# First pair of a hash-attention kernel: the queries' hash products moved ahead of the keys' transposes, and the first key block's scores cut into equal halves

## The chip, the cores and the metric

The kernel runs on one core of one Trainium2 chip. The time is the device time of one execution in microseconds (us); a kernel's time is the median of several executions. The profile is one execution recorded by the hardware profiler; its times start at the first instruction.

The engines are named as in the profile: PE is TensorE's matrix multiplication and PEld its weight load, DVE is VectorE, ACT is ScalarE, POOL is GpSimd, SP is SyncE, which here only issues transfers.

## The reference

Attention over hash buckets (4 batches, 8 heads, 768 positions, head size 64), and behind it two dense layers with a squared ReLU between them. A query sees only the keys of its own bucket; the bucket is made of the signs of six products with `proj`.

```python
def _attn_ref(q, k, v, proj):
    ...
    q_bits = (np.einsum('bhsd,dk->bhsk', q, proj) > 0).astype(np.int64)
    k_bits = (np.einsum('bhsd,dk->bhsk', k, proj) > 0).astype(np.int64)
    ...
    mask = q_bucket[:, :, :, None] == k_bucket[:, :, None, :]
    scores = scale * np.matmul(q, k.transpose(0, 1, 3, 2))
    scores = np.where(mask, scores, -1000000000.0)
    scores = scores - np.max(scores, axis=-1, keepdims=True)
    attn = np.exp(scores)
    attn = attn / (np.sum(attn, axis=-1, keepdims=True) + 1e-09)
    return np.matmul(attn, v)

def _moe_ref(x, w_in, w_out):
    r = np.maximum(x @ w_in, 0.0)
    return (r * r) @ w_out
```

All inputs and the output are float32.

## The kernel before

The attention comes first, in 16 pairs of heads (`NP`). Each pair works on tiles of 128 partitions: head 0 of the pair lies on partitions 0 to 63, head 1 on 64 to 127. A pair has 768 queries and 768 keys; the keys are taken in six blocks of 128 (`kt`, 0 to 5). The two dense layers follow and make up most of the time. The order of the instructions on every engine is the order of the program's text: the whole of it stands under a manual schedule, and each engine works off its own queue.

What happens for one pair:

- `features` (or, for pair 0 alone, `first_features`) brings queries and keys into the form with the head's 64 numbers on partitions, `feat`. For pair 0 it is done by TensorE: three transposes of 128x128 into one tile `tp` for each half of 384 positions, copied out by ScalarE for the queries (`w == 0`, line 316) and by VectorE for the keys (`w == 1`, line 318).
- `hash_bits` multiplies `feat` by `projs` (line 346), for one half of 384 positions (`c`) and one head (`h`) at a time. It is float32, and each product shows as two passes in the trace. `projs` holds `proj` twice, once for each head; the two halves are loaded on SP's and ScalarE's queues behind the queries and keys of pair 0 (line 277).
- `signs` turns the products into query bits on ScalarE (line 356, four instructions, in the order half 0 head 0, half 0 head 1, half 1 head 0, half 1 head 1). The keys of pair 0 get theirs on VectorE, in `first_keys` (two comparisons at line 370, one multiply-add at line 374), one half of 384 keys at a time.
- `score(pr, kt)` multiplies one block of 128 keys by all queries (line 396): a product of features in float32 and a product of bits in bfloat16 into the same PSUM tile `st`, cut by `CUTS` into 512 and 256 queries. One exponential for each cut (line 413) writes the weights `e`, for both heads at once, so 1024 and 512 elements per partition. For the very first block the feature products of both cuts are issued first and the bit products behind them; in all others a cut's bits come first and its features next.
- `add_up`, `attend`, `sum_up` and `normalize` sum the weights, multiply them by the values and divide.

PSUM tiles come from a pool of three (`turn`): transposes, hash products and scores share them, and whoever asks for one waits until its last reader is done. The queries' hash products of pair 0 go instead into the tile `void` that `keep_busy` writes. `keep_busy` issues matmuls of a constant, eight ahead of the first transposes and two ahead of the keys' transposes.

Before the loop over the pairs the order was, on TensorE: eight matmuls of `keep_busy`, the queries' transposes (both halves), two matmuls of `keep_busy`, the transposes of key half 0, the queries' hash products, the hash products of key half 0, the transposes of key half 1. Then `score(0, 0)`, the hash of key half 1 (`first_keys(1, ...)`), `score(0, 1)`, and so on. On VectorE: the copy of key half 0, the three instructions for its bits, the copy of key half 1, then the bits of half 1, and then the transposes for pair 1.

Of the kernel before, what the change touches and what calls it, by code (L numbers as in the profile page):

```python
# [34 lines left out]
def kernel(  # L35
# [13 lines left out]
    B, H, S, D = q.shape  # L49
# [5 lines left out]
    HS = S // 2  # L55
# [5 lines left out]
    CUTS = (0, 512), (512, S)  # L61
# [42 lines left out]
    def turn(name):  # L104

        return ps_s.tile([P, 2, 512], FP32, name=name, tag="turn")
# [195 lines left out]
    def first_features(w, r):  # L302

        if r == 0:
            feat[0, w] = p_f.tile([P, S], FP32, name=f"feat{w}")
        tp = turn("tp")[:, 0]
        for i in range(SB // 2):
            t = r * (SB // 2) + i
            nc.tensor.transpose(  # L309
                out=tp[:, i * P:(i + 1) * P],  # L310
                in_=nat[0, ("q_nat", "k_nat")[w]][:, t].rearrange("p h d -> p (h d)"),
                identity=ident,
            )
        out = feat[0, w][:, r * HS:(r + 1) * HS]
        if w == 0:
            nc.scalar.copy(out=out, in_=tp[:, 0:HS])
        else:
            nc.vector.tensor_copy(out=out, in_=tp[:, 0:HS])

    busy = const.tile([P, 512], BF16, name="busy")  # L320
    void = ps_o.tile([P, 1024], FP32, name="xo")

    def keep_busy(n, w=512):

        for _ in range(n):
            nc.tensor.matmul(  # L326
                out=void[:, 0:w], lhsT=busy[:, 0:P], rhs=busy[:, 0:w], start=True, stop=True
            )
# [8 lines left out]
    def hash_bits(pr, banks, ws=(0, 1), cs=(0, 1)):  # L337


        for w in ws:  # L340
            hashed[pr, w] = banks
            for c in cs:
                g = 2 * w + c
                for h in range(2):
                    rows = slice(h * D, (h + 1) * D)
                    nc.tensor.matmul(  # L346
                        out=banks[g * NR_B:(g + 1) * NR_B, h, 0:HS], lhsT=projs[rows],
                        rhs=feat[pr, w][rows, c * HS:(c + 1) * HS], start=True, stop=True,
                    )

    def signs(pr, w):
        bits[pr, w] = t = all_bits[pr % 2][w]
        for c in range(2):
            at = slice((2 * w + c) * NR_B, (2 * w + c + 1) * NR_B)
            for h in range(2):
                nc.scalar.activation(  # L356
                    out=t[h * D:h * D + NR_B, c * HS:(c + 1) * HS], in_=hashed[pr, w][at, h, 0:HS],
                    func=ACTF.Sign, scale=HUGE, bias=lifts[at],
                )
# [26 lines left out]
    def score(pr, kt):  # L386

        e = ring[len(weights) % NRING]
        weights[pr, kt] = e
        key = slice(kt * P, (kt + 1) * P)  # L390
        sts = []

        def products(st, lo, hi, src, first):
            for h in range(2):
                rows = slice(h * D, (h + 1) * D)
                nc.tensor.matmul(  # L396
                    out=st[:, h, 0:hi - lo], lhsT=src[pr, 1][rows, key],
                    rhs=src[pr, 0][rows, lo:hi], start=first, stop=not first,
                )


        if (pr, kt) == (0, 0):
            for lo, hi in CUTS:
                sts.append(turn("st"))
                products(sts[-1], lo, hi, feat, True)
        for i, (lo, hi) in enumerate(CUTS):
            if len(sts) <= i:
                sts.append(turn("st"))
                products(sts[i], lo, hi, bits, True)
                products(sts[i], lo, hi, feat, False)  # L410
            else:
                products(sts[i], lo, hi, bits, False)
            nc.scalar.activation(  # L413
                out=e[:, :, lo:hi], in_=sts[i][:, :, 0:hi - lo], func=ACTF.Exp, scale=scale
            )
# [176 lines left out]
    with tc.manual_schedule():  # L592
# [10 lines left out]
        first_features(0, 0)  # L603
        first_features(0, 1)
        keep_busy(2)
        first_features(1, 0)
        hash_bits(0, void.rearrange("p (h c) -> p h c", h=2), (0,))
        signs(0, 0)
        first_keys(0, turn("hash"))
        first_features(1, 1)  # L610
# [3 lines left out]
        for pr in range(NP):  # L614
# [17 lines left out]
            if pr > 0:  # L632
                round_weight(b - 2)
                load_weight(b)
                for m in sums.get(pr, ()):
                    sum_in(m)
            score(pr, 0)
            if pr == 0:
                first_keys(1, turn("hash"))
            score(pr, 1)  # L640
            if pr == 0:
                for w in range(2):
# [8 lines left out]
            if pr == X_0 + 1:  # L651
                for n in range(2):
                    load_unit(n)
            part_weight(a)
            score(pr, 2)
            if pr == 0:
                prepare()
# [826 lines left out]
```

## Time and profile before

| | us |
|---|---|
| time, median of 4 runs | 878.47 |
| lowest and highest of them | 878.12, 879.19 |
| the profiled execution's own time | 878.54 |
| its span, first to last instruction | 876.8 |
| outside the span | 1.74 |
| PE busy between 13.0 and 28.6 us | 14.12 of 15.6 |
| ACT busy between 13.0 and 28.6 us | 14.85 of 15.6 |
| PE busy from 28.6 us to the end | 839.43 of 848.2 |

A line of the timeline gives the start, the duration, the engine, the source line, the operation, the tile written and those read, the shape, the count, and in brackets how long the engine was idle before it and what ended that idle time. Lines that follow each other closely are merged. The chain of waits is found backwards from the last instruction: at every step it goes to what released it. The end of a matmul is modelled by the profiler, and a wait for several things is charged to the one that seems to have come last.

### The profile page before, as it was taken

Reading aid. Unit: us, or ns where it says so; the run is one execution under the profiler, and the core shown is the slowest. Engines: PE = TensorE matmul, PEld = TensorE weight load, DVE = VectorE, ACT = ScalarE, POOL = GpSimd, SP = SyncE. Lnnn points to the kernel's source line nnn. Section 1 sums busy time; section 2 is a strip of 40 time slices with the busy share of each in tenths; the row PEclk is TensorE's granted clock in tenths of the full one; section 3 lists DMA queues with packets and bytes.
Section 4 is the critical chain, followed back from the end, with each engine's and each line's share of the span. In section 5 each row is a group of like instructions: output and inputs, shape, how many; then the busy total and the mean of one; then the engine's idle time right before and its main releaser. Section 6 shows DMA issues by size and latency. Waiting matters only on the chain.

```text
span 876.8 us, 12130 instructions
## 1 busy us (share of the span) xinstructions
PE 864.8 (99%) x4340; PEld 519.6 (59%) x4340; DVE 760.1 (87%) x1099; ACT 391.8 (45%) x673; POOL 107.4 (12%) x172
## 2 busy tenths in 40 slices
PE   8999999999999999999999999999999999999996
PEld 4444444444444444444688865556888755568885
DVE  5999999999999998888689978888889788888875
ACT  6988888888888851222211123332111233321110
POOL 2000000000000000554032021111000211110002
PEclk9999999999999999999999999999999999999999
DMA  9877967998888536999788874536756754355565
GB/s 169 151 150 133 234 155 153 183 258 223 180 179 218 167 102 213 297 265 285 296 297 259 219 169 160 175 121 222 282 157 182 166 166 154 124 168 158 154 178 102
DMA packets 224131, 167.09 MB, mean 191 GB/s; under 512 B 164448, under 2 KB 181344, under 8 KB 224064
## 3 DMA queue, kind: packets, MB, share of 16 engines
q1 hardware_dynamic: 189152, 87.19, 41.4%
q0 software_dynamic: 12528, 41.30, 15.4%
q10 hardware_dynamic: 22384, 37.76, 14.1%
q8 instruction: 36, 0.59, 0.3%
q14 instruction: 31, 0.25, 0.1%
HBM read 124.52 MB, written 41.68 MB: 190 GB/s over the span
## 4 chain that ended last, share of the span: by engine, by line
PE 96%; DVE 2%; ACT 1%; issue 0%; DVEq 0%; ACTq 0%
PE acc L712 40%; PE st L396 17%; PE acc L931 16%; PE xo L438 14%; PE acc L884 6%; PE hash L346 2%; PE tot L455 1%; DVE total L428 1%; ACT bits L356 1%; PE xo L326 0%; ACT e L413 0%; PE tp L309 0%; PE xo L477 0%; PE xo L346 0%; DVE x_t L493 0%
## 5 line engine op out<-in xcount | busy, mean ns | idle before, releaser
L413 ACT ACTIVATE e<-st 128x1024 f32<-128x1024 f32 x192 | 145.0, 810 | 44.8 <-PE st L396 41.0
L396 PE MATMUL st<-feat,feat 64*128 64x512 f32 (+1 forms) x768 | 150.4, 483 | 0.0
L438 PE MATMUL xo<-e,v_nat 128*64 128x512 f32 (+1 forms) x768 | 134.8, 492 | 0.0
L712 PE MATMUL acc<-b,leaf 128*128 128x256 f32 x600 | 132.9, 379 | 0.0
L712 PEld LDWEIGHTS acc<-b,leaf 128*128 128x128 f32 x600 | 113.9, 190 | 16.0 <-issue 0.6
L428 DVE TENSOR_TENSOR total<-total,e 128x1536 f32<-128x1536 f32 x64 | 112.4, 1756 | 8.2 <-ACT e L413 3.6
L438 PEld LDWEIGHTS xo<-e,v_nat 128*64 128x64 f32 x768 | 51.3, 136 | 82.2 <-issue 74.3
L931 PE MATMUL acc<-t_x,w_unit 128*128 128x512 f32 x192 | 90.2, 592 | 0.0
L396 PEld LDWEIGHTS st<-feat,feat 64*128 64x128 f32 x768 | 66.0, 188 | 32.8 <-issue 23.2
L712 PE MATMUL acc<-t,leaf 128*128 128x256 f32 x336 | 76.2, 380 | 0.0
L356 ACT ACTIVATE bits<-hash,lifts 32x384 bf16<-32x384 f32 x120 | 68.7, 573 | 2.3 <-PE hash L346 0.5
L712 PEld LDWEIGHTS acc<-t,leaf 128*128 128x128 f32 x336 | 63.6, 190 | 9.1 <-DVE t L516 0.5
L796 DVE SCALAR_TENSOR_TENSOR b<-h 128x512 f32<-128x512 f32 x96 | 65.7, 691 | 3.0
L396 PE MATMUL st<-bits,bits 64*128 64x256 bf16 (+1 forms) x384 | 63.2, 325 | 1.7 <-ACT e L413 1.2
L931 PE MATMUL acc<-x,w_unit 128*128 128x512 f32 x128 | 60.1, 592 | 0.0
L712 PE MATMUL acc<-x,w_unit 128*128 128x512 f32 x128 | 56.6, 594 | 0.0
L712 PE MATMUL acc<-b_t,leaf 128*128 128x256 f32 x240 | 53.8, 379 | 0.0
L931 PEld LDWEIGHTS acc<-t_x,w_unit 128*128 128x128 f32 x192 | 36.5, 190 | 28.9 <-issue 26.8
L719 ACT COPY two<-acc 128x256 f32<-128x256 f32 (+1 forms) x29 | 12.5, 432 | 87.7 <-PE acc L712 78.4
L719 ACT COPY one<-acc 128x256 f32<-128x256 f32 (+1 forms) x29 | 12.5, 431 | 84.2 <-PE acc L712 55.4
L712 PEld LDWEIGHTS acc<-b_t,leaf 128*128 128x128 f32 x240 | 45.5, 190 | 6.2
L396 PEld LDWEIGHTS <-bits 64*128 64x128 bf16 x384 | 23.6, 93 | 42.7 <-issue 38.6
(159 smaller groups left out, 1167.3 us busy)
## 6 DMA issues: line engine op xcount, KB each, us to landing
leaf<-w_out ACTq DMA_DIRECT2D x142, 256.0 KB, 3.1
w_unit<-w_in SPq DMA_DIRECT2D x16, 640.0 KB, 4.0
raw<-in_moe_w_in_dram SPq DMA_DIRECT2D x16, 512.0 KB, 5.5
raw<-in_moe_w_out_dram SPq DMA_DIRECT2D x16, 512.0 KB, 4.3
w_unit<-w_in SPq DMA_DIRECT2D x8, 896.0 KB, 8.1
w_out<-sums POOLq DMA_DIRECT2D x16, 448.0 KB, 6.9
sum<-w_in SPq DMA_DIRECT2D x16, 448.0 KB, 5.0
v_nat<-in_v_dram SPq DMA_DIRECT2D x16, 384.0 KB, 4.4
```

Of the source, the lines that this page charges most:

```text
L346: nc.tensor.matmul(out=banks[g * NR_B:(g + 1) * NR_B, h, 0:HS], lhsT=projs[rows], rhs=feat[pr, w][rows, c * HS:(c + 1) * HS], start=True, ...
L356: nc.scalar.activation(out=t[h * D:h * D + NR_B, c * HS:(c + 1) * HS], in_=hashed[pr, w][at, h, 0:HS], func=ACTF.Sign, scale=HUGE, bias=li ...
L396: nc.tensor.matmul(out=st[:, h, 0:hi - lo], lhsT=src[pr, 1][rows, key], rhs=src[pr, 0][rows, lo:hi], start=first, stop=not first,)
L413: nc.scalar.activation(out=e[:, :, lo:hi], in_=sts[i][:, :, 0:hi - lo], func=ACTF.Exp, scale=scale)
L428: nc.vector.tensor_tensor(out=totals[pr], in0=totals[pr], in1=weights[pr, kt][:, :, 0:S], op=ALU.add)
L438: nc.tensor.matmul(out=xo[h * D:(h + 1) * D, lo:hi], lhsT=nat[pr, "v_nat"][:, h, kt * D:(kt + 1) * D], rhs=weights[pr, kt][:, h, lo:hi], s ...
L455: nc.tensor.matmul(out=tot[g * 32:(g + 1) * 32, 0:HS], lhsT=ones, rhs=totals[pr][:, h, c * HS:(c + 1) * HS], start=True, stop=True,)
L712: nc.tensor.matmul(out=acc[to], lhsT=a(i), rhs=b(i), start=first and i == 0, stop=last and i == n - 1, skip_group_check=True,)
L719: nc.scalar.copy(out=t, in_=acc[of])
L796: nc.vector.scalar_tensor_tensor(out=out, in0=h, scalar=0.0, in1=h, op0=ALU.max, op1=ALU.mult)
L884: nc.tensor.matmul(out=out, lhsT=w[:, a], rhs=b, start=start, stop=stop, skip_group_check=True)
L931: nc.tensor.matmul(out=acc[to], lhsT=w[:, PLACE[a], f], rhs=bt[b](f), start=first and f == 0, stop=last and f == NFT // 2 - 1, skip_group_ ...
```

## The change

Two edits, both for pair 0 alone.

First, the call that makes the queries' hash products is moved up by one: it now stands ahead of the transposes of key half 0 instead of behind them. Nothing is added or left out; on TensorE four products change places with three transposes, and no other engine's order changes.

Second, the first key block (`kt` 0 of pair 0) is scored in two halves of 384 queries instead of 512 and 256. The four feature products, the four bit products and the two exponentials of that block have 384 columns (768 elements for an exponential) each. All other blocks keep `CUTS`. With it two waits for PSUM tiles change places in key block 1 and 2: the second tile of block 1 now waits for the second exponential of block 0, and the first tile of block 2 for VectorE's reading of the hash of key half 1; before, it was the other way about.

```diff
@@ score @@
+        cuts = CUTS
         if (pr, kt) == (0, 0):
-            for lo, hi in CUTS:
+            cuts = (0, HS), (HS, S)
+            for lo, hi in cuts:
                 sts.append(turn("st"))
                 products(sts[-1], lo, hi, feat, True)
-        for i, (lo, hi) in enumerate(CUTS):
+        for i, (lo, hi) in enumerate(cuts):
             if len(sts) <= i:
                 sts.append(turn("st"))
                 products(sts[i], lo, hi, bits, True)
...
         first_features(0, 0)
         first_features(0, 1)
         keep_busy(2)
+        hash_bits(0, void.rearrange("p (h c) -> p h c", h=2), (0,))
         first_features(1, 0)
-        hash_bits(0, void.rearrange("p (h c) -> p h c", h=2), (0,))
         signs(0, 0)
         first_keys(0, turn("hash"))
         first_features(1, 1)
```

`HS` is 384 and `S` is 768.

## The prediction

> **What bounds the kernel now.** I read the page first (busy shares and the chain that ended last), then the chain of waits in order of time for the stretch the change touches, then the timeline of the same stretch, and last the tile `projs`, because the moved products read it.
>
> ```profile
> span 876.8 us, 12130 instructions
> PE 864.8 (99%) x4340; PEld 519.6 (59%) x4340; DVE 760.1 (87%) x1099; ACT 391.8 (45%) x673; POOL 107.4 (12%) x172
> ...
> PE 96%; DVE 2%; ACT 1%; issue 0%; DVEq 0%; ACTq 0%
> ```
>
> TensorE is the bound: 99% busy, 96% of the chain. The edits add no work to it, so they count only through when the first scores are ready.
>
> ```profile
> 6.72 0.36 PE tp L309 x3
> 7.09 1.05 PE xo L346 x8
> 8.13 0.44 PE hash L346 x4
> 8.58 0.48 PE tp L309 x3
> 9.05 1.98 PE st L396 x10
> 11.03 0.02 issue
> 11.05 1.03 ACT e L413
> 12.09 0.04 issue
> 12.13 3.41 PE st L396 x24
> ...
> 21.27 1.51 ACT e L413 x2
> ```
>
> This is the chain from 6.72 to 22.78 us. Up to 12 us one thing follows another: key transposes, hash products, scores, first exponential. From 12.13 the exponentials and signs carry it (ScalarE is busy 14.85 of the 15.60 us between 13.0 and 28.6), and from 25.16 on it is TensorE to the end. No load interrupts that chain. So if the first exponential starts later, everything behind starts later by what reaches 12.13, unless a later wait has room.
>
> ```profile
> 6.54 0.31 PEld L309 LDWEIGHTS tp<-ident,k_nat 128*128 128x128 f32 x3 [0.31 <-DMA k_nat<-in_k_dram]
> 7.04 0.40 PEld L346 LDWEIGHTS xo<-feat,projs 64*32 64x32 f32 x8 [0.19 <-ACT feat L316]
> 7.13 0.56 DVE L318 COPY feat<-tp 128x384 f32<-128x384 f32 x1 [3.84 <-PE tp L309]
> 8.25 2.35 ACT L356 ACTIVATE bits<-xo,lifts 32x384 bf16<-32x384 f32 x4 [1.44 <-PE xo L346]
> 8.51 0.31 PEld L309 LDWEIGHTS tp<-ident,k_nat 128*128 128x128 f32 x3 [0.62 <-PE xo L346]
> 9.86 0.38 DVE L374 TENSOR_SCALAR bits<-bits,spans,bases 128x384 bf16<-128x384 bf16 x1
> 9.88 0.30 PEld L396 LDWEIGHTS st<-feat,feat 64*128 64x128 f32 x4 [0.59 <-DVE bits L370]
> 10.41 0.71 PE L396 MATMUL st<-bits,bits 64*128 64x512 bf16 x4
> ```
>
> Columns: start, duration, engine, line, operation, count, idle time before and its releaser. Line 1: the first key transposes start as `k_nat` lands. Line 2: the queries' products start at 7.04; the bracket blames ScalarE's copy, but the two copies ran 5.75 to 6.81 and were long done. The late one is a load:
>
> ```profile
> 1.86 0.58 SPq L277 DMA_DIRECT2D projs<-in_proj_dram  x1
> 1.99 0.57 ACTq L277 DMA_DIRECT2D projs<-in_proj_dram  x1
> DMA to landing us min/median/max: 5.1/5.2/5.3
> ```
>
> Issued at 1.86 and 1.99, landing 5.1 and 5.3 us later: 6.96 and 7.29. The products of head 0 need the first, those of head 1 the second (weight loads start at 7.04 and 7.29). The key transposes now lie wholly in that wait (6.54 to 7.09).
>
> **The change part by part.** *Products ahead of transposes.* TensorE issues in the program's order, so the three key transposes, ready at 6.54, go behind four products (eight passes) that cannot start before 7.04. The products gain nothing: `projs` lands when it did. They start their last pass at 7.65 as before, and the signs still run 8.25 to 10.60. The transposes' place: behind the other hash products, the last pass started at 8.09 and the transposes' weight load at 8.51, 0.42 later. I take that row: 7.65 + 0.42 = 8.07 instead of 6.54, +1.53. The lower bound is the row where scores follow transposes (8.78 to 8.98, 0.20): 7.85, +1.31.
>
> The Trainium skill, "TensorE: Matmul & The Clock Gate", Part 2 (step-by-step), says weight loads are pulled ahead of matmuls in flight when row groups don't conflict or the background buffer is free. By it the transposes could start soon after 7.65, some 0.4 us earlier, and the estimate would be 879.3; the row of 8.51 shows the load held back although the semaphore it is charged to came at the products' end, so the row is taken.
>
> What is queued behind the transposes moves with them, on TensorE and VectorE. Copy of key half 0: 7.13 to 8.65. Hash of that half: 7.74 to 9.27. Key bits ready: 9.86 + 0.38 = 10.24, so 11.77. Second transposes, first score products and VectorE's second copy move by the same 1.53 (copy ends 10.83, so 12.36). ScalarE's queue keeps its times until the exponential. No DMA moves: SP's queue has neither edit in it, and its transfers that wait for pair 0's buffers are issued from 11.45 and 18.04, the transposes being over at 10.6.
>
> *Halves.* The first key block is scored as 384 + 384 instead of 512 + 256: as many matmuls, columns and activations. The second score tile waits for the bank of the key hash, freed by VectorE: 9.88 + 1.53 = 11.41. Its passes are 384 columns instead of 256. A 512-column pass is 0.43 long (start to start), so 384 take 0.32; the first one behind fresh weights took 0.10 more (8.98 to 9.52). The bit products start at 11.41 + 0.42 + 0.32 = 12.15, behind the key bits of 11.77, so here TensorE decides. A bit product lasts 0.38 at 512 columns and 0.27 at 256, so 0.32: done 12.47, exponential at 12.50 instead of 11.05, +1.45. The signs (10.60) no longer hold it.
>
> Here the halves give something back. The first exponential has 768 elements instead of 1024. No row shows 768; the bounds are 0.59 (512) and 1.03 (1024), and I take the middle, 0.81. It frees its bank at 13.31, and the next scores start at 13.36 instead of 12.13: +1.23. The hash of key half 1 lies in between: 12.15 + 0.32 = 12.47, last pass 0.35 later and 0.32 long, so over by 13.15, hidden with 0.2 to spare. Without that cover (0.59 for the exponential) it would decide and the shift be about 1.0. At 1.03 it is 1.45.
>
> Two waits change place. The second tile of key block 1 now waits for the second exponential (12.50 + 1.51 = 14.01; needed 13.20 + 1.23 = 14.43), and the first of block 2 for VectorE's reading of the second key hash (13.07 + 1.41 = 14.48; needed 13.75 + 1.23 = 14.98). Both have 0.4 or more to spare: nothing. VectorE's transposes for pair 1 end 15.24 + 1.41 = 16.65; pair 1's hash wants them at 15.50 + 1.23 = 16.73. That costs nothing, but with under 0.1 to spare.
>
> **Sum:** -0 (products not earlier) + 1.53 (transposes) - 0.08 (signs no longer awaited, TensorE now) - 0.22 (shorter first exponential) = +1.23 on the profiled execution's 878.54, so 879.77. Its time is 0.07 above the median 878.47, so 879.7 for a median. With the bounds, +0.8 to +1.6: 879.2 to 880.1 is the forecast's own range.
>
> **Rivals.**
> *A, the keys land last (not slower).* If `k_nat` landed 1.5 us later, at 8.07 or after, the transposes would lose nothing by standing behind the products, and only the halves would act. Key bits are ready at 10.24, the first half starts 10.41, exponential at 10.77 instead of 11.05: -0.3, 878.2. For it: these loads land 3.7 to 5.2 us after issue, a wide spread. Against: in the trace the keys came 0.45 before the first `projs`, and `projs` is issued behind them on the same two queues. 8%.
> *B, the delay is swallowed later.* There are idle stretches on TensorE at 20.81 (0.48), 24.16 (0.99) and a hold for VectorE near 32.4 (0.27). Against: the first two wait for ScalarE, which shifts too; the third waits for a VectorE queue that itself waited for an exponential at 22.8. 878.5; 6%.
> *C, the delay grows (clearly slower).* The spare of under 0.1 us at pair 1's transposes fails and every bound is at its far end: first exponential 1.03, VectorE 1.45 late plus 0.3 to 0.5 of waits that no longer interlock. +1.8 to 2.2: 880.5. For it: VectorE is busy without a break from 13.0 to 17. Against: each step has its row. 17%.
> *D, TensorE falls to half pace.* At the start, 512-column matmuls of `busy` are 0.42 apart, and 0.21 from 6.13 on. The change opens idle stretches at 6.72 to 7.07 and 8.65 to 9.27. If they brought the slow pace back, some 3 us of passes between 9.27 and 14 would double: +4.2, 882.7. Against: after the idle 0.99 us before 25.16 passes run at the same pace as before it. The granted clock shows 1.00 throughout, the slow start included, so only durations can tell. 5%.
>
> **How the numbers follow.** Forecast 64%, A 8%, B 6%, C 17%, D 5%. The predicted time is the forecast's, 879.7. What a measurement of this kernel can tell from no change is 0.2%, 1.76 us: faster needs under 876.7, slower over 880.2. The forecast, A and B lie between; so "same" though I expect a real loss of about 0.14%. Slower: C's larger part, D, and a few per cent of the forecast's tail, 22%. Faster has no mechanism larger than 0.3 us: 2%. The range 878.6 to 881.0 holds forecast, C, and part of A and B.
>
> **What would show it.** In the changed profile: the queries' products still start near 7.04 and their signs near 8.25 (first step); the first key transposes load at about 8.07 and VectorE copies at 8.65 (second); bit products near 12.15, behind VectorE's 11.77 (third); a first exponential of 0.81 at 12.50 and the next scores at 13.36 (fourth); pair 1's signs at 16.58 + 1.23 = 17.8 and TensorE's unbroken run from 26.4 instead of 25.16. It would be wrong if `projs` landed earlier, if the transposes didn't wait for the products, or if a shift seen at 13.4 were gone at 26.

## The result, and the profile after

The changed kernel takes 880.05 us (median of 39 runs, 879.40 to 880.93) against 878.69 us (59 runs) before: ratio 1.0015, 95% interval 1.0011 to 1.0020, so 1.0 to 1.8 us slower. The profiled execution took 879.65 us with a span of 877.9, against 878.54 and 876.8: 1.1 us more.

The page of the changed kernel, engines' busy time and the chain that ended last:

```profile
span 877.9 us, 12130 instructions
PE 864.9 (99%) x4340; PEld 519.1 (59%) x4340; DVE 760.1 (87%) x1099; ACT 391.5 (45%) x673; POOL 107.1 (12%) x172
...
PE 96%; DVE 2%; ACT 1%; DMA 1%; issue 0%; DVEq 0%; ACTq 0%
```

No engine has more work than before: as many instructions, TensorE's busy time up by 0.1 us. What is new is a share of 1% for a transfer in the chain, which had none. The chain of waits of the changed kernel, in order of time (start, duration, what), shows which:

```profile
1.86 5.07 DMA projs<-in_proj_dram
6.93 0.14 issue
7.07 1.04 PE xo L346 x8
8.11 0.49 PE tp L309 x3
8.60 0.02 issue
8.63 0.57 DVE feat L318
9.19 0.04 issue
9.24 0.84 PE hash L346 x4
...
13.38 3.41 PE st L396 x24
...
26.40 0.72 PE st L396 x6
```

The chain now begins with the load of `projs`, goes through the queries' products and only then comes to the key transposes. Before, transposes ran 6.72 to 7.08 on this chain and the products followed. The second score stretch starts at 13.38 instead of 12.13, and the run of TensorE that lasts to the end at 26.40 instead of 25.16.

From the timeline of the same stretch, changed kernel (lines between these are left out):

```profile
7.04 0.38 PEld L346 LDWEIGHTS xo<-feat,projs 64*32 64x32 f32 x8 [1.26 <-ACT feat L316]
7.07 1.04 PE L346 MATMUL xo<-feat,projs 64*32 64x384 f32 x8 [0.79 <-DMA projs<-in_proj_dram]
8.04 0.31 PEld L309 LDWEIGHTS tp<-ident,k_nat 128*128 128x128 f32 x3 [0.62 <-issue]
8.22 2.36 ACT L356 ACTIVATE bits<-xo,lifts 32x384 bf16<-32x384 f32 x4 [1.81 <-issue]
8.63 0.56 DVE L318 COPY feat<-tp 128x384 f32<-128x384 f32 x1 [5.34 <-PE tp L309]
11.36 0.38 DVE L374 TENSOR_SCALAR bits<-bits,spans,bases 128x384 bf16<-128x384 bf16 x1
12.13 0.49 PE L396 MATMUL st<-bits,bits 64*128 64x384 bf16 x4
12.52 0.81 ACT L415 ACTIVATE e<-st 128x768 f32<-128x768 f32 x1 [1.94 <-PE st L396]
12.55 0.83 PE L346 MATMUL hash<-feat,projs 64*32 64x384 f32 x4
13.31 0.16 PEld L396 LDWEIGHTS <-bits 64*128 64x128 bf16 x2 [0.62 <-issue]
13.38 0.39 PE L396 MATMUL st<-bits,bits 64*128 64x512 bf16 x2
...
15.79 0.94 DVE L333 STREAM_TRANSPOSE feat<-k_nat 128x768 f32<-128x768 f32 x1
...
16.72 0.91 PE L346 MATMUL hash<-feat,projs 64*32 64x384 f32 x16
```

The first two lines carry the result: moved to the front, the products start when they started before, 7.04, and TensorE sits idle for 0.79 us ahead of them, released by the landing of `projs`. That time held the key transposes. Everything from line 3 on is late, apart from the signs (8.22 against 8.25).

Where does the delay go afterwards? Matching the VectorE instructions of the two traces one to one gives a clean answer: the changed kernel is 1.24 us late at 24.5 us, 1.23 at 53, 1.23 at 158, 1.23 at 313, 1.22 at 415 and 1.22 at 827. The delay of the first pair is carried to the last VectorE instruction at 869 us without gain or loss; only behind it is 0.1 us made up, so that the spans differ by 1.1. The second trace of both edits carries its 1.42 us unchanged to 450 us, and then 0.2 us come in (see the last section). It had been expected that the delay would reach the dense layers unchanged to within 0.05 us, whatever the loads add: so far as the attention goes that held, beyond it it did not.

### The profile page after: what moved, and what is told of

Read it like the earlier page. It is cut to its first block, busy times and chain, and to the rows that moved or that the text cites. A ratio compares the mean times of both kernels' runs of the same rounds, so it can differ in the third digit from the quotient of the medians.

```text
span 877.9 us, 12130 instructions
## 1 busy us (share of the span) xinstructions
PE 864.9 (99%) x4340; PEld 519.1 (59%) x4340; DVE 760.1 (87%) x1099; ACT 391.5 (45%) x673; POOL 107.1 (12%) x172
## 4 chain that ended last, share of the span: by engine, by line
PE 96%; DVE 2%; ACT 1%; DMA 1%; issue 0%; DVEq 0%; ACTq 0%
PE acc L714 40%; PE st L396 17%; PE acc L933 16%; PE xo L440 14%; PE acc L886 6%; PE hash L346 2%; PE tot L457 1%; DVE total L430 1%; DMA projs<-in_proj_dram 1%; ACT bits L356 1%; ACT e L415 0%; PE xo L479 0%; PE xo L346 0%; DVE x_t L495 0%; DVE recs L489 0%
## 5 line engine op out<-in xcount | busy, mean ns | idle before, releaser
L415 ACT ACTIVATE e<-st 128x1024 f32<-128x1024 f32 (+1 forms) x192 | 145.1, 810 | 46.1 <-PE st L396 42.3
L396 PE MATMUL st<-feat,feat 64*128 64x256 f32 (+2 forms) x768 | 150.6, 484 | 0.0
L396 PE MATMUL st<-bits,bits 64*128 64x256 bf16 (+2 forms) x384 | 63.0, 325 | 1.4 <-ACT e L415 1.0
```

The costliest lines, as they stand in the source:

```text
L396: nc.tensor.matmul(out=st[:, h, 0:hi - lo], lhsT=src[pr, 1][rows, key], rhs=src[pr, 0][rows, lo:hi], start=first, stop=not first,)
L415: nc.scalar.activation(out=e[:, :, lo:hi], in_=sts[i][:, :, 0:hi - lo], func=ACTF.Exp, scale=scale)
```

## The experiments

In all tables "next scores" is the start of the first exponential of key block 1, the instruction that started at 13.42 us in the profile before and at 14.67 with the change; the "next scores" of the prediction are TensorE's, which began 1.29 us earlier in both (12.13 and 13.38). "Key transposes load" is the start of their first weight load. "Against before" is the difference of the medians, with the 95% interval of the ratio put into us.

| run | key transposes load | next scores | against before, us |
|---|---|---|---|
| before | 6.54 | 13.42 | |
| both edits | 8.04 | 14.67 (+1.25) | +1.36 (1.0 to 1.8) |
| both edits, again | 8.21 | 14.85 (+1.43) | +1.30 (0.5 to 2.1) |
| order alone | 8.09 | 14.77 (+1.35) | +1.19 (0.4 to 2.0) |
| halves alone | 6.84 | 13.73 (+0.31) | +0.06 (-0.6 to 1.0) |
| projs between, new order | 7.72 | 14.35 (+0.93) | +0.65 (0.0 to 1.6) |
| projs between, old order | 7.57 | 14.20 (+0.78) | +0.63 (-0.2 to 1.4) |
| keys' transposes together | 6.69 | 13.20 (-0.22) | +0.12 (-0.4 to 1.1) |
| the same, no halves | 6.67 | 13.62 (+0.20) | +0.44 (-0.4 to 1.2) |
| keys loaded first | 4.56 | 14.26 (+0.84) | +0.55 (-0.3 to 1.3) |
| projs on GpSimd, new order | 8.74 | 15.37 (+1.95) | +1.90 (1.1 to 2.7) |
| projs on GpSimd, old order | 6.82 | 13.69 (+0.27) | +0.30 (-0.6 to 1.0) |
| the same, keys' transposes together | 6.60 | 13.64 (+0.22) | +0.08 (-0.7 to 0.9) |
| no load of projs, new order | 7.28 | 13.91 (+0.49) | +0.25 (-0.4 to 1.2) |

The intervals are wide against the effects, so most verdicts below rest on the traces, where a start is known to 0.01 us, and the medians only say whether they fit. But there is one trace of each kernel, and executions differ: the two of both edits are 0.18 us apart at the next scores.

### Each edit alone

Order alone:

```diff
-        first_features(1, 0)
         hash_bits(0, void.rearrange("p (h c) -> p h c", h=2), (0,))
+        first_features(1, 0)
```

> The queries' hash products ahead of the keys' transposes, the first block in 512 and 256 as before. Theory (the transposes stand behind products that wait for projs, and the halves give a little back): first key transposes load near 8.05 us instead of 6.54, key bits 1.5 us later, next scores (12.13 before) near 13.6, as nothing shortens the first exponential: +1.4 to +1.5 us, so slightly worse than both edits together. Rival (the halves cost, the order is free because projs is late anyway): no change, within 0.3 us of before.

Halves alone is the changed kernel with these two lines put back.

> The first block in two halves of 384, the old order. Theory: the first exponential starts near 10.98 instead of 11.05 and is 0.81 instead of 1.03 long, the next scores start near 11.85 instead of 12.13, and pair 1's signs near 16.3 instead of 16.58: -0.25 to -0.3 us. Rival (the halves cost): +0.5 us or more, because the second tile's 128 more columns stand ahead of the bit products.

The order costs nearly everything by itself: +1.19 us, +1.35 in the trace, just under the expected 1.4 to 1.5. The rival, that the order is free, falls. But the theory had the halves give back 0.2, and of that little is left. Order alone, ScalarE:

```profile
12.41 1.51 ACT L413 ACTIVATE e<-st 128x1024 f32<-128x1024 f32 x2 [1.79 <-PE st L396]
```

Without the halves the first exponential starts at 12.41, although the loads came 0.05 us later than in the trace of both edits, where it starts at 12.52. The second score tile is a third shorter (256 columns instead of 384), so the bit products come earlier; the halves lose at the start of the exponential some 0.15 of the 0.22 us that they win by its length.

Halves alone measures no difference, 0.25 us being below what eleven runs tell. Its trace has the keys late by themselves:

```profile
6.84 0.57 PEld L309 LDWEIGHTS tp<-ident,k_nat 128*128 128x128 f32 x3 [0.40 <-DMA k_nat<-in_k_dram]
...
7.68 0.56 DVE L318 COPY feat<-tp 128x384 f32<-128x384 f32 x1 [4.41 <-PE tp L309]
...
13.73 2.65 ACT L415 ACTIVATE e<-st 128x1024 f32<-128x1024 f32 x3 [0.64 <-PE st L396]
```

The keys landed 0.30 us later than in the profile before (weights load at 6.84 against 6.54), and three transposes' weight loads took 0.57 instead of 0.31 us, since TensorE still ran at its slow pace. So VectorE's copy is 0.55 late (7.68 against 7.13), but the next scores only 0.31: from the copy on, the halves win 0.24 in the old order, as expected. One trace of each shows it; the medians don't.

### Which load comes first

Both kernels load `projs` between the queries and the keys of pair 0; the first has both edits, the second the halves and the old order.

```diff
             nat[0, name] = t
-        for h, queue in enumerate((nc.sync, nc.scalar)):
-            queue.dma_start(out=projs[h * D:(h + 1) * D, 0:NBITS], in_=proj)
+            if name == "q_nat":
+                for h, queue in enumerate((nc.sync, nc.scalar)):
+                    queue.dma_start(out=projs[h * D:(h + 1) * D, 0:NBITS], in_=proj)
```

> Both edits, and projs loaded between pair 0's queries and keys instead of behind the keys. Theory (of the 1.5 us by which the transposes are late, the wait for projs is 0.5): projs lands near 5 us, the products start near 6.4 to 6.8, the transposes at 7.4 to 7.8, if the keys have landed by then; the time is 0.3 to 0.7 us under that of both edits, so +0.6 to +1.0 against before. Rival (the load's place is of no account, the order of matrix work alone costs): same time as with both edits, +1.2 to +1.4.

> Halves, old order, and projs loaded between pair 0's queries and keys. Theory: the key transposes start when the keys land, now 0 to 0.7 us later than 6.54; the products follow without a wait. So -0.3 to +0.4 us against before, and the two orders differ by 0.4 to 1.1 us under this order of loads, against some 1.5 us under the old one. Rival (order of matrix work alone): the two orders still differ by 1.5 us.

The weight loads of the key transposes, new order and then old order:

```profile
7.72 0.31 PEld L310 LDWEIGHTS tp<-ident,k_nat 128*128 128x128 f32 x3 [0.76 <-DMA k_nat<-in_k_dram]
```

```profile
7.57 0.31 PEld L310 LDWEIGHTS tp<-ident,k_nat 128*128 128x128 f32 x3 [1.62 <-DMA k_nat<-in_k_dram]
```

In both the bracket now names the keys' load: `projs` lands near 5 us (3.1 to 3.7 after its issue at 1.49), and the keys about 1 us later than before, since their issue moved from 1.28 to 2.12. With the keys last the order of the matrix work is nearly free: the two kernels differ by 0.02 us in the medians and by 0.15 in the next scores, where under the old load order it is over 1 us. This is the prediction's rival A brought about on purpose: the keys land last (at 7.5 to 7.6, not at 8.07 as it asked, but `projs` is early too), and the order's cost goes. The new order's +0.65 lies in the expected 0.6 to 1.0, but partly by luck: its transposes waited for the keys, not for the products. That the old order would stay between -0.3 and +0.4 was a miss; it measured +0.63, because I had put the keys' lateness at 0.7 at most.

### How late projs is

Three kernels load `projs` on GpSimd's queue, right behind the identity matrix.

```diff
         make_identity(nc, ident)
+        for h in range(2):
+            nc.gpsimd.dma_start(out=projs[h * D:(h + 1) * D, 0:NBITS], in_=proj)
```

> Both edits, and projs loaded on GpSimd's queue right behind the identity, so without a place behind the queries and keys; the loads of queries and keys keep their queues. It takes the wait for projs out of the new order. Theory (the 1.5 us by which the key transposes are late are 0.53 of wait for projs, 0.58 of products, 0.42 until the transposes' weights load): if projs lands by 6, the products start near 6.4 to 6.7, the transposes 1.0 later, near 7.5, and the next scores are late by 0.6 to 0.8 instead of 1.23: +0.6 to +0.9 us. Rival (the whole cost is the wait for projs): no loss against before. Second rival (the wait costs nothing): +1.2 to +1.4 as with both edits.

> Halves, old order, projs on GpSimd's queue. Theory: the key transposes start when the keys land (about 6.5 to 6.8) and the products directly behind them; key bits as before or 0.1 earlier, the halves give 0.25: -0.2 to -0.4 us against before. If the order were free once projs is early, it would be equal to the run before this one; the theory has them 0.9 to 1.1 us apart.

> Halves, both halves of the keys transposed ahead of the products, projs on GpSimd's queue. Theory: as the run before it and 0.1 to 0.2 us better, since the second transposes and VectorE's second copy leave the stretch ahead of the first scores: -0.4 to -0.5 us, unless the keys land late. Rival (the second transposes now stand ahead of the products, which no longer wait): +0.2 us against the run before it.

All three expectations stood on an early landing and were missed, for it was later: issued at 1.78 and 2.48, landed 5.4 to 5.9 us after. The new order, timeline:

```profile
7.62 1.20 PE L344 MATMUL xo<-feat,projs 64*32 64x384 f32 x8 [0.77 <-DMA projs<-in_proj_dram]
7.97 0.15 PEld L344 LDWEIGHTS xo<-feat,projs 64*32 64x32 f32 x6 [0.25 <-DMA projs<-in_proj_dram]
8.74 0.31 PEld L307 LDWEIGHTS tp<-ident,k_nat 128*128 128x128 f32 x3 [0.62 <-issue]
```

The run tests the opposite of what was meant: a `projs` that comes still later. Head 1's weights load at 7.97 instead of 7.27, 0.70 us later, and the key transposes at 8.74 instead of 8.04, 0.70 later, and the next scores 0.70 later (15.37 against 14.67). Under the new order a late `projs` is passed on in full. The second trace of both edits has the same on a smaller scale (transposes 0.17 later, next scores 0.18). In the old order the same late load leaves the next scores at +0.27, though there too the chain of waits now runs through that load.

Then the load was taken away: `projs` is filled with the constant 0.5 in its six columns, so the buckets are not the reference's.

```diff
         nc.vector.memset(projs, 0.0)
+        nc.vector.memset(projs[:, 0:NBITS], 0.5)
-        for h, queue in enumerate((nc.sync, nc.scalar)):
-            queue.dma_start(out=projs[h * D:(h + 1) * D, 0:NBITS], in_=proj)
```

> Both edits, with projs filled with the constant 0.5 in place of proj, so no load of it at all: the buckets are not the reference's, the work on every engine is the same. It takes the wait for projs wholly out of the new order. Theory (1.53 us of delay = 0.53 wait + 0.58 products + 0.42 until the transposes' weights load): products start between 6.3 and 6.9, as ScalarE's copies end; transposes between 7.2 and 7.6, no longer tied to projs; offset of the dense layers +0.5 to +0.8 us instead of +1.23 to +1.41, time +0.5 to +0.9. If the whole cost is the wait: transposes at the keys' landing (6.5 to 6.8), time at or under that of before. If the wait costs nothing: +1.2 or more.

```profile
6.25 0.40 PEld L344 LDWEIGHTS xo<-feat,projs 64*32 64x32 f32 x8 [0.42 <-ACT feat L314]
...
7.28 0.31 PEld L307 LDWEIGHTS tp<-ident,k_nat 128*128 128x128 f32 x3 [0.62 <-DMA k_nat<-in_k_dram]
```

Now the products start at 6.25, on ScalarE's copies, and the transposes at 7.28: 0.76 of the delay at the transposes goes with the wait (7.28 against 8.04), and as much at the next scores (13.91 against 14.67). What stays, 0.49, is the products themselves and the pause behind them: the transposes still stand behind eight passes. (Their bracket names the keys' load, but it had landed by 6.7.) So neither "the whole cost is the wait" nor "the wait costs nothing" holds. The median, +0.25, is below the expected 0.5 to 0.9; its interval, -0.4 to 1.2, takes in the trace's 0.49, and no change as well, so this rests on the trace.

### Towards a better order

The first puts the second half's transposes into the wait for `projs`, with the halves; the second does the same without them.

```diff
         first_features(1, 0)
+        first_features(1, 1)
         hash_bits(0, void.rearrange("p (h c) -> p h c", h=2), (0,))
         signs(0, 0)
         first_keys(0, turn("hash"))
-        first_features(1, 1)
```

> Halves, and both halves of the keys transposed ahead of the queries' products, so in the wait for projs. Theory (work put into that wait costs nothing, and the second transposes and VectorE's second copy leave the stretch between the key hash and the first scores): if the keys land as in the profile of before, key bits stay at 10.24, the first exponential is at 10.77 instead of 11.05, the next scores at 11.65 instead of 12.13: -0.4 to -0.5 us, 0.2 better than halves alone. Rival (the first stretch is set by the loads' landing and nothing else): no change against halves alone.

> The same order with 512 and 256 in the first block. Theory: bit products at 10.41 to 10.65, held by VectorE's key bits (10.24) and ScalarE's signs (10.60) as before, so the first exponential stays at 11.05 and the time at that of before, within 0.15 us; what the free TensorE could give is only to be had with the halves. Rival: the transposes moved give 0.4 us by themselves.

The third also loads, transposes and hashes the keys ahead of the queries.

```diff
-        for src, name in ((q, "q_nat"), (k, "k_nat")):
+        for src, name in ((k, "k_nat"), (q, "q_nat")):
...
-        first_features(0, 0)
-        first_features(0, 1)
-        keep_busy(2)
         first_features(1, 0)
+        first_features(1, 1)
+        keep_busy(2)
+        first_features(0, 0)
+        first_features(0, 1)
+        first_keys(0, turn("hash"))
         hash_bits(0, void.rearrange("p (h c) -> p h c", h=2), (0,))
         signs(0, 0)
-        first_keys(0, turn("hash"))
-        first_features(1, 1)
```

> Halves, and the keys loaded, transposed, copied and hashed ahead of the queries; the queries' half-0 bits are enough for the first half. Theory (the keys' way to their bits is the longer one, so it should get the earlier load): key bits at 9.6 instead of 10.24, first exponential near 10.2 to 10.3, next scores near 11.1 instead of 12.13: -0.8 to -1.0 us. Rival (the queries' signs take over, as they start later): signs of half 0 end near 10.0 and hold the bit products: -0.3 to -0.5 us.

The first has the earliest next scores of all runs, 13.20, with keys that landed 0.15 later than in the profile before: half of the expected gain of 0.4 to 0.5. In the median it is told neither from before (+0.12) nor from halves alone. The second was to stay at the time of before; its first exponential came 0.21 later (11.26 for 11.05), and its +0.44 has too wide an interval to tell. The third is a plain miss. ScalarE, first kernel and then third:

```profile
8.47 2.36 ACT L356 ACTIVATE bits<-xo,lifts 32x384 bf16<-32x384 f32 x4 [1.58 <-PE xo L346]
10.93 1.51 ACT L415 ACTIVATE e<-st 128x768 f32<-128x768 f32 x2
```

```profile
9.53 2.36 ACT L356 ACTIVATE bits<-xo,lifts 32x384 bf16<-32x384 f32 x4 [0.99 <-issue]
11.91 1.51 ACT L415 ACTIVATE e<-st 128x768 f32<-128x768 f32 x2
```

Signs from 9.53 for 2.36 us end at 11.89, and the exponential starts 0.02 later without idle time; in the first kernel the two are 0.10 apart (10.83, 10.93). The halves need only the first two signs, but ScalarE works in order and the exponential stands behind all four. I had counted the bits of half 0 and not the queue.

But the exponential is not what makes the third kernel late. Its timeline and its chain of waits have TensorE and VectorE in that place:

```profile
10.06 1.56 PE L396 MATMUL st<-feat,feat 64*128 64x384 f32 x8 [0.64 <-DVE bits L370]
11.46 0.80 PE L396 MATMUL st<-bits,bits 64*128 64x384 bf16 x4
```

```profile
9.45 0.57 DVE bits L370
...
10.06 2.19 PE st L396 x12
12.26 0.77 PE hash L346 x4
13.03 3.34 PE st L396 x24
```

The first score products start at 10.06, released by VectorE's second comparison of the key hash, where the first kernel has them at 8.66. Their bit products for the first half end at 11.79, so without the signs the exponential could have started some 0.1 us earlier. Why the score products wait for that comparison was not looked into. The signs cost more at another place: the last of the four bit products needs the last sign. It starts 0.05 us behind it in both kernels (10.89 and 11.94), and the hash of key half 1 and the next scores stand behind it in TensorE's queue. The kernel with `projs` on GpSimd and the keys' transposes together has that wait in plain sight:

```profile
11.29 1.51 ACT L413 ACTIVATE e<-st 128x768 f32<-128x768 f32 x2
11.32 0.32 PE L394 MATMUL st<-bits,bits 64*128 64x384 bf16 x1 [0.16 <-ACT bits L354]
```

So keys that are ready earlier meet the signs, and no run here beats the kernel before in the median.

## Why the prediction was right

- **What bounds.** Right: first scores late, everything behind late by the same amount to the end.
- **The products gain nothing.** Right, and the decisive step: 7.04 and 8.22 were measured for 7.04 and 8.25. The bracket of the profile before named ScalarE's copy; the landing times of `projs` gave the real release. After the change the profile itself names the load.
- **The transposes, +1.53.** 8.04 for 8.07. Its parts by experiment: without the load 0.76 of it goes; what was taken for the wait was 0.53. That was counted from the keys' landing, but without the load the products start ahead of it, at 6.25, as ScalarE's copies ended 0.34 us earlier there (6.46) than in the profile before (6.80).
- **VectorE's chain, +1.53.** Key bits ready at 11.74 for 11.77.
- **Halves.** Bit products 12.13 for 12.15, exponential 12.52 for 12.50 and 0.81 long for 0.81 (the bounds were 0.59 and 1.03), TensorE's next scores at 13.38 for 13.36. But calling 0.22 a gift of the halves was misleading: in the new order the longer second tile takes most of it back, and the order alone costs about what both do. The sum counted both (the 384 columns are in its 12.15), the words only the gain. And the hash of key half 1 was not hidden with 0.2 to spare: behind its last pass (12.89) comes the same pause of 0.4 that was reckoned with for the transposes, and the prediction left it out here. The weights of the next scores load at 13.31, and the scores start at 13.38, so a shorter exponential could have won 0.07 at most. The shift came out because the exponential still ended last, by that little: some luck.
- **Waits that change place, pair 1's hash with under 0.1 to spare.** No cost: pair 1's signs at 17.82 for 17.8, TensorE's run from 26.40 for 26.4. But the spare was used up: VectorE was 1.49 late and not 1.41, and its transposes ended at 16.73 (worked out: 16.65) as the hash began, at 16.72.
- **Size.** +1.23 was worked out, +1.25 is in the trace, and the medians say +1.36 (1.0 to 1.8). The time is 880.05 for 879.7: 0.22 of the difference is the median before, 878.47 from four runs and 878.69 from 59, and 0.13 the change. The profiled execution before was 0.15 below that median and not 0.07 above it, perhaps because its keys landed at 6.50 and in most traces since at 6.6 to 6.8. And 0.15% was told from no change after all, with 59 and 39 runs, where the prediction had put the least that can be told at 0.2%.
- **Rivals.** A's condition did not hold; when the loads were swapped the keys did land last. B: nothing was swallowed. C: no wait grew, though one came to its edge (above). D: passes behind the idle stretches run at full pace, a hash pass pair again 0.35 after the first.

The Trainium skill, "TensorE: Matmul & The Clock Gate", Part 2, has weight loads pulled ahead of matmuls in flight, when the row groups don't conflict or the load goes to the background weight buffer. In the trace of the change the load came late: the last product started at 7.63, the transposes' weight load at 8.04, with the keys landed before and no semaphore named ("issue"). The traces don't show whether the page's conditions were met. The pause of 0.41 is there in every trace with the new order in which the keys had landed by then (five of six).

## What to carry to other kernels

Before moving work ahead in a queue that runs in order, find what the moved work waits for, from landing times and not from the bracket alone; if it waits for a load, the queue stands still and what used to fill the gap pays. In a prologue, order the work by the landing of its inputs. And when a consumer is cut in halves to start earlier, look whether the queues still put it, or what follows it, behind the whole producer.

## What the runs showed that was not expected

TensorE's pace doubles at a moment that differs from one execution to the next. The six transposes of the first operand, second trace of both edits and then order alone:

```profile
4.74 0.83 PE L309 MATMUL tp<-ident,q_nat 128*128 128x128 f32 x6
```

```profile
4.87 1.48 PE L309 MATMUL tp<-ident,q_nat 128*128 128x128 f32 x6
```

The same work takes 0.83 or 1.48 us; in the run that loads the keys first the slow pace lasts to about 7.3. The granted clock shows 1.00 in this stretch in all of them. The Trainium skill, "TensorE: Matmul & The Clock Gate", Part 1, has the change at about 4 us of activity, give or take 0.5; here it came from 3.2 to 5.8 us after the first matmul at 1.48, a wider spread.

A transfer of 1.5 KB on a queue of its own is no faster. On GpSimd's queue `projs` took 5.4 to 5.9 us to land, behind the queries and keys on the other two queues 5.0 to 5.5, and 3.1 to 3.7 ahead of the keys. The Trainium skill, "Trainium Kernel Development and Optimization", Key Constraints, says that transfers from all these queues run on the same 16 DMA engines; these landings agree with it, but no run here tells that from a slower start of GpSimd's queue.

The dense layers are not always equally long: against the trace of the kernel before, 0.1 to 1.1 us come in in nine of the thirteen others at one to three places between 330 and 640 us, the same few places in several kernels. What causes it was not looked into; it is a part of the medians' scatter.
